# The Gram of a linear-attention kernel on two column halves of the array: groups of three heads, state in two PSUM banks

## The chip, the cores and the metric

The kernel runs on one core of one Trainium2 chip. The metric is the device time of one execution in microseconds (us), as the median of several. All executions quoted were with a granted TensorE clock of 1.0.

In this document PE is TensorE (matmul), PEld is TensorE's weight load, which overlaps PE, DVE is VectorE and ACT is ScalarE. "L434" is line 434 of the kernel that the profile belongs to. An edit shifts line numbers, so the Gram is L434 in the kernel before, L436 in the changed one.

## The reference, cut to what matters

Two branches of the same input x (2048 tokens, width 640) are mixed by a gate. Branch B is a feed-forward net (width 1728) with GELU. Branch A is linear attention with 32 heads of 20 channels:

```python
phi_q = concat([softmax(q @ w_phi), softmax(-q @ w_phi)])   # 40 features a head
phi_k = concat([softmax(k @ w_phi), softmax(-k @ w_phi)])
kv  = einsum("bhsf,bhsd->bhfd", phi_k, v)     # the state; summed over all tokens
z   = einsum("bhsf->bhf", phi_k)
num = einsum("bhqf,bhfd->bhqd", phi_q, kv)
den = einsum("bhqf,bhf->bhq", phi_q, z) + 1e-6
o   = num / den
```

The change concerns the state (kv, z), which the kernel calls the Gram: 16 tiles of 128 tokens, accumulated in PSUM.

## The kernel before

A one is appended to each head's 20 values, so v has 21 columns a head and z comes out with kv. `Ek` holds both halves of phi_k, `vaug` the values. Six heads (6 x 21 = 126 columns of v) form one group, and one matmul computes all 6 x 6 head pairs; only the diagonal blocks are of use. The rest is masked away later.

```python
NSE = 4        # slots of Ek
def gram_groups(self):
    fe = 6 * self.DH                                   # 120 features of six heads
    for g in range(6):
        lo = min(6 * g * self.DA, self.H * self.DA - P)
        yield g, 3 + g % 2 if g < 4 else 5, 2 * fe * (g // 2 if g < 4 else g - 4), lo, fe * g, min(fe, self.D - fe * g)

def gram(self, t):
    ...
    for g, b, c, lo, f0, nf in self.gram_groups():
        sc.op("pe", lambda e: e.matmul(
            self.bank(b)[:, c:c + 2 * nf], va[:, lo:lo + P], self.Ek[:, se, :, f0:f0 + nf],
            start=(t == 0 and g in (0, 1, 4)), stop=..., skip_group_check=True), ...)
```

One tile is six matmuls with weights 128x128: five stream 240 columns, one 80. They stand between other matmuls of the attention stage. The same loop issues key and value projections, `k_norm` on DVE (the softmax normalisation that the Gram needs), and the query projections `pq`:

```python
for t in range(4, NT):
    if t < 8: self.k_early(t, 1)
    else:     self.vk(t)
    self.k_norm(t)
    m = 2 * t - 2 if t < 8 else t + 5
    while n < m:
        if n == m - 1:
            for g in range(g, t - 2 if t < 8 else t - 1):
                self.gram(g)
            g = t - 2 if t < 8 else t - 1
        self.pq(order[n][0], order[n][1], n)
        n += 1
```

Tile 0's Gram is issued before this loop. The last two (14 and 15) stand among the first feed-forward matmuls. Tile 15 is followed by `kv_evac` (PSUM to SBUF, then a transposing DMA) and, three feed-forward chunks later, by `kv_mask` (DVE). `num` uses the result. Tiles 5 and 6 fall into the same iteration, so there are 15 bursts of Gram matmuls for 16 tiles.

The softmax here doesn't subtract the row's maximum and nothing guards it: scores larger than these inputs give would overflow.

Of the kernel before, what the change touches and what calls it, by code (L numbers as in the profile page):

```python
# [3 lines left out]
P = 128  # L4
# [101 lines left out]
class _Kernel:  # L106
# [314 lines left out]
                  reads=[("Rk", se)], writes=[("Ek", se, s)])  # L421

    def gram_groups(self):
        fe = 6 * self.DH
        for g in range(6):
            lo = min(6 * g * self.DA, self.H * self.DA - P)
            yield g, 3 + g % 2 if g < 4 else 5, 2 * fe * (g // 2 if g < 4 else g - 4), lo, fe * g, min(fe, self.D - fe * g)

    def gram(self, t):
        sc = self.sc  # L430
        se, sv = t % self.NSE, t % self.NSV
        va = self.vaug[:, sv, :, :].rearrange("p h c -> p (h c)")
        for g, b, c, lo, f0, nf in self.gram_groups():
            sc.op("pe", lambda e: e.matmul(  # L434
                self.bank(b)[:, c:c + 2 * nf], va[:, lo:lo + P], self.Ek[:, se, :, f0:f0 + nf],
                start=(t == 0 and g in (0, 1, 4)), stop=(t == self.NT - 1 and g in (2, 3, 5)), skip_group_check=True),  # L436
                reads=[("Ek", se, 0), ("Ek", se, 1), ("vaug", sv), ("vmain", sv), ("vone", sv)], writes=[("ps", b)],
                signal=(g in (2, 3, 5)))

    def kv_evac(self):  # L440
        sc = self.sc
        fe = 6 * self.DH

        def copy(ek, dst, src, rd, wr):
            if ek == "d":
                sc.op("dve", lambda e: e.tensor_copy(dst, src), reads=rd, writes=wr)
            else:
                sc.op("act", lambda e: e.activation(dst, src, AF.Copy), reads=rd, writes=wr)
        for pl, ek in ((0, "d"), (1, "a")):
            f = pl * fe  # L450
            dst = self.Ek[:, pl, :, 0:4 * fe].rearrange("p s (b c) -> p b s c", c=2 * fe)[:, :, :, f:f + fe]
            src = self.bank(3 + pl, 4 * fe).rearrange("p (b s f) -> p b s f", f=fe, s=2)
            copy(ek, dst, src, [("ps", 3 + pl)], [("Ek", pl, 0)])
        for pl, ek in ((0, "d"), (1, "d")):
            g = 4 + pl
            nf = min(fe, self.D - fe * g)
            src = self.bank(5)[:, pl * 2 * fe:pl * 2 * fe + 2 * nf].rearrange("p (s f) -> p s f", f=nf)
            copy(ek, self.Ek[:, pl, :, fe * g:fe * g + nf], src, [("ps", 5)], [("Ek", pl, 1)])
        for pl in (0, 1):
            sc.dma("sp", lambda e: e.dma_start_transpose(  # L460
                self.Ek[:, 2 + pl, :, :].rearrange("p s (i c) -> p (s i) c", c=P),
                self.Ek[:, pl, :, :].rearrange("p s f -> p (s f)")),
                reads=[("Ek", pl, 0), ("Ek", pl, 1)], writes=[("Ek", 2 + pl, 0), ("Ek", 2 + pl, 1)])

    def kv_mask(self):
        sc = self.sc
        self.kvk = {i: [] for i in range(self.KD)}
        lows = {g: lo for g, b, c, lo, f0, nf in self.gram_groups()}
        for i in range(self.KD):
            for g in range(self.HLO[i] // 6, self.HHI[i] // 6 + 1):  # L470
                h0, h1 = max(self.HLO[i], 6 * g), min(self.HHI[i], 6 * g + 5)
                nh, j0 = h1 - h0 + 1, h0 - self.HLO[i]
                o = i * P + h0 * self.DA - lows[g]
                dst = self.KV[:, i, :, j0 * self.DB:(j0 + nh) * self.DB].rearrange(
                    "p s (h c) -> p s h c", c=self.DB)[:, :, :, 0:self.DA]
                src = self.Ek[:, 2 + g % 2, :, o:o + nh * self.DA].rearrange("p s (h c) -> p s h c", c=self.DA)
                m = self.mask[:, i, j0:j0 + nh].unsqueeze(1).unsqueeze(3).to_broadcast([P, 2, nh, self.DA])
                sc.op("dve", lambda e: e.tensor_tensor(dst, src, m, ALU.mult),
                      reads=[("Ek", 2 + g % 2, 0), ("mask", i), ("KVd", i, 0), ("KVd", i, 1)], writes=[("KV", i, g)])
                self.kvk[i].append(("KV", i, g))  # L480

    def pq(self, b, i, n):
# [338 lines left out]
```

## Time and profile before

The median was 296.51 us over three runs (296.28 to 296.85).

| what | reading |
|---|---|
| PE busy, whole span | 98% |
| chain of waits | 93% PE |
| Gram's share of that chain | 3%, 15 bursts, 8.8 us |
| PE busy, 30 to 84 us | 54.00 of 54.00 us |

These are the engines' busy times on the page of the kernel before:

```profile
PE 291.0 (98%) x1904; PEld 169.1 (57%) x1904; DVE 162.7 (55%) x321; ACT 104.2 (35%) x183; POOL 27.8 (9%) x56
```

The chain of waits is the work that ended last, followed back from the last instruction, at each step to what released it. That of the kernel before, in order of time, follows: start in us, duration in us, engine, tile, line, number of instructions. L486 is `pq`, L341 the projections, L434 the Gram, L594 the feed-forward up-projections, L709 the output copy.

```profile
29.64 1.25 PE ps L486 x5
30.89 0.55 PE ps L434 x6
31.44 1.08 PE ps L486 x5
...
48.79 2.71 PE ps L341 x15
51.50 1.10 PE ps L434 x12
52.60 1.08 PE ps L486 x5
...
60.72 0.55 PE ps L434 x6
61.27 1.08 PE ps L486 x5
...
294.23 0.37 ACT outsb L709
```

From 29.64 us to the last output copy at 294.23 us, the chain is unbroken PE work (but for 0.02 us at its very end), 264.59 us long. Whatever the Gram saves there is saved in full, provided that nothing else becomes the limit. A tile costs 0.55 us (24 of these matmuls in a row took 2.19 us in experiment 3), so all 16 cost 8.76 us. A `pq` group after it takes 1.08 us, its ordinary duration.

The trace already holds matmuls in another tiling mode: the half chunk of the feed-forward (L672, weights of 64 rows, two at once on the array's row halves). These lines, again from the chain of the kernel before, price a change of mode. L699 is the output projection that follows.

```profile
119.86 0.38 PE ps L672 x4
120.24 1.46 PE ps L699 x10
...
125.93 1.36 PE ps L699 x10
...
172.98 0.65 PE ps L672 x8
```

Four more row-tiled matmuls cost 0.65 - 0.38 = 0.27 us, so a pair takes 0.135 us. The first two pairs therefore include 0.38 - 0.27 = 0.11 us for getting into the mode. The next ten full matmuls take 1.46 us in place of 1.36: another 0.10 us for getting out.

DVE's normalisation is close to being a second limit. In the timeline of DVE in the kernel before (start, duration, engine, line, operation, shapes), these are tile 6's two normalising multiplications:

```profile
50.19 1.56 DVE L420 TENSOR_TENSOR Ek<-Ek,Dk 128x640 bf16<-128x640 bf16 x2
```

They end at 51.75 us, and tile 6's Gram is the second half of the 1.10 us burst that starts at 51.50, so it starts at 52.05 us: 0.3 us of slack.

### The profile page before, as it was taken

How to read it: one execution, taken by the hardware profiler on the slowest of the kernel's cores; microseconds unless marked ns; L12 is line 12 of the kernel's file. 1: busy time of each engine (PE TensorE's matmuls, PEld its weight loads, DVE VectorE, ACT ScalarE, POOL GpSimd, SP SyncE). 2: the span in 40 equal slices, each digit the busy share in tenths (PEclk: the TensorE clock that was granted, in tenths of full speed). 3: DMA queues.
4: the chain of work that ended last, by engine and by line, in shares of the span. 5: the costliest groups of instructions: out<-in, count | busy, mean ns of one | idle time of the engine just before them, and what ended most of it. 6: DMA issues, size and time to landing. Idle time of an engine off the chain costs nothing.

```text
span 296.1 us, 4789 instructions
## 1 busy us (share of the span) xinstructions
PE 291.0 (98%) x1904; PEld 169.1 (57%) x1904; DVE 162.7 (55%) x321; ACT 104.2 (35%) x183; POOL 27.8 (9%) x56
## 2 busy tenths in 40 slices
PE   7989999999999999999999999999999999999997
PEld 3656565555554455766555567655556765555674
DVE  3238999998886579600777710077771007777100
ACT  3347787766773221112222211222221122222112
POOL 7000000000000011110111100012110001222000
PEclk9999999999999999999999999999999999999999
DMA  8999993000001302211011130101311000111111
GB/s 231 181 200 273 364 356 113 0 0 2 0 2 31 57 4 37 51 47 44 3 23 22 24 44 22 46 0 23 24 22 43 25 26 21 22 22 24 22 46 44
DMA packets 38224, 18.85 MB, mean 64 GB/s; under 512 B 30266, under 2 KB 37946, under 8 KB 38202
## 3 DMA queue, kind: packets, MB, share of 16 engines
q1 hardware_dynamic: 37392, 18.19, 25.0%
q10 hardware_dynamic: 810, 0.35, 0.4%
q8 instruction: 15, 0.25, 0.4%
q14 instruction: 7, 0.06, 0.1%
HBM read 9.04 MB, written 2.62 MB: 39 GB/s over the span
## 4 chain that ended last, share of the span: by engine, by line
PE 93%; SPq 3%; DMA 2%; ACT 1%; issue 0%; ACTq 0%
PE ps L594 38%; PE ps L693 19%; PE ps L341 12%; PE ps L699 8%; PE ps L486 7%; PE ps L630 4%; PE ps L434 3%; DMA xT<-in_A_x_dram 2%; SPq L213 2%; PE ps L604 1%; PE ps L672 1%; PE ps L321 1%; SPq L217 1%; SPq L226 1%; ACT Ek L400 0%; ACT Eq L492 0%
## 5 line engine op out<-in xcount | busy, mean ns | idle before, releaser
L599 DVE TENSOR_TENSOR hT<-ps,gl 128x512 bf16<-128x512 f32 x52 | 35.7, 688 | 79.8 <-PE ps L594 79.7
L594 PE MATMUL ps<-xT,wg_sb 128*128 128x512 bf16 x260 | 64.6, 379 | 0.0
L594 PE MATMUL ps<-xT,wu_sb 128*128 128x512 bf16 x260 | 64.6, 379 | 0.0
L597 ACT ACTIVATE gl<-ps 128x512 bf16<-128x512 f32 x52 | 31.1, 597 | 82.5 <-PE ps L594 80.3
L693 PE MATMUL ps<-wd_sb,hT 128*128 128x320 bf16 (+2 forms) x416 | 59.3, 299 | 0.0
L693 PEld LDWEIGHTS ps<-wd_sb,hT 128*128 128x128 bf16 x416 | 40.2, 98 | 16.8
L659 POOL TENSOR_TENSOR Og<-O,O 128x640 bf16<-128x640 bf16 x16 | 22.3, 1396 | 244.4 <-DVE O L657 244.4
L594 PEld LDWEIGHTS ps<-xT,wu_sb 128*128 128x128 bf16 x260 | 25.4, 98 | 30.7
L341 PE MATMUL ps<-w,xT 128*128 128x512 bf16 (+3 forms) x240 | 41.0, 321 | 1.4 <-DMA xT<-in_A_x_dram 1.4
L594 PEld LDWEIGHTS ps<-xT,wg_sb 128*128 128x128 bf16 x260 | 24.9, 98 | 26.4
L709 ACT ACTIVATE outsb<-ps,Gm 128x640 bf16<-128x640 f32 (+2 forms) x17 | 13.0, 763 | 71.5 <-PE ps L699 71.5
L341 PEld LDWEIGHTS ps<-w,xT 128*128 128x128 bf16 x240 | 22.3, 97 | 19.7 <-DMA xT<-in_A_x_dram 1.6
L411 DVE TENSOR_REDUCE Dk<-Ek 128x64 f32<-128x1280 bf16 x16 | 23.7, 1480 | 3.2 <-ACT gcol L403 3.2
L420 DVE TENSOR_TENSOR Ek<-Ek,Dk 128x640 bf16<-128x640 bf16 x32 | 25.0, 821 | 0.6
L486 PE MATMUL ps<-xT,wq 128*128 128x512 bf16 x100 | 24.7, 379 | 0.3 <-ACT Eq L492 0.3
L657 DVE TENSOR_TENSOR O<-ps,RH 128x640 bf16<-128x640 f32 x32 | 24.8, 815 | 0.0
L699 PE MATMUL ps<-wo_sb,goT 128*128 128x320 bf16 (+2 forms) x160 | 24.6, 299 | 0.0
L492 ACT ACTIVATE Eq<-ps 128x512 bf16<-128x512 f32 x40 | 21.7, 604 | 4.0 <-PE ps L486 4.0
L400 ACT ACTIVATE Ek<-ps 128x640 bf16<-128x640 f32 x32 | 20.7, 702 | 3.5 <-PE ps L341 3.5
L699 PEld LDWEIGHTS ps<-wo_sb,goT 128*128 128x128 bf16 x160 | 15.1, 98 | 7.2 <-issue 1.3
L630 PEld LDWEIGHTS ps<-KV,Eq 128*128 128x128 bf16 x192 | 12.0, 98 | 3.6
L630 PE MATMUL ps<-KV,Eq 128*128 128x154 bf16 x192 | 13.7, 221 | 0.0
(63 smaller groups left out, 148.4 us busy)
## 6 DMA issues: line engine op xcount, KB each, us to landing
out_dram<-outsb SPq DMA_DIRECT2D x15, 160.0 KB, 1.8
wd_sb<-in_B_w_down_dram SPq DMA_DIRECT2D x1, 2080.0 KB, 13.7
wg_sb<-in_B_w_gate_dram SPq DMA_DIRECT2D x1, 1120.0 KB, 6.1
wu_sb<-in_B_w_up_dram SPq DMA_DIRECT2D x1, 1120.0 KB, 8.5
wg_sb<-in_B_w_gate_dram SPq DMA_DIRECT2D x1, 960.0 KB, 9.8
wu_sb<-in_B_w_up_dram SPq DMA_DIRECT2D x1, 960.0 KB, 10.2
w<-in_A_wqkv_dram SPq DMA_DIRECT2D x5, 160.0 KB, 4.2
wo_sb<-in_A_wo_dram SPq DMA_DIRECT2D x1, 800.0 KB, 9.2
```

The costliest lines, as they stand in the source:

```text
L341: sc.op("pe", lambda e, kt=kt: e.matmul(self.bank(bank)[:, bcol:bcol + n], self.xT[:, kt, t * P:(t + 1) * P], self.w3[:, kt, c0:c0 + n], s ...
L411: sc.op("dve", lambda e: e.tensor_reduce(self.Dk[:, se, 0, :].rearrange("p (s h) -> p s h", h=H), self.Ek[:, se, :, :].rearrange("p s (h d ...
L420: sc.op("dve", lambda e, v=v, r=r: e.tensor_tensor(v, v, r, ALU.mult), reads=[("Rk", se)], writes=[("Ek", se, s)])
L486: sc.op("pe", lambda e, kt=kt: e.matmul(self.bank(bank), self.wq2[:, kt, i * P:(i + 1) * P], self.xT[:, kt, b * self.BT:(b + 1) * self.BT] ...
L594: sc.op("pe", lambda e, kt=kt, w=w, bk=bk: e.matmul(self.bank(bk), w[:, kt, c * P:(c + 1) * P], xs(kt), start=(kt == 0), stop=(kt == self. ...
L597: sc.op("act", lambda e: e.activation(self.gl[:, slot, :], self.bank(banks[0]), AF.Gelu_apprx_tanh), reads=[("ps", banks[0])], writes=[("g ...
L599: sc.op("dve", lambda e: e.tensor_tensor(self.hT[:, c, :], self.bank(banks[1]), self.gl[:, slot, :], ALU.mult), reads=[("ps", banks[1]), ( ...
L630: sc.op("pe", lambda e, s=s, i=i, n=n, o0=o0, k0=k0, bk=bk, r=r: e.matmul(self.bank(bk)[:, o0:o0 + n], self.Eq[:, s, i, t * P:(t + 1) * P] ...
L657: dve(lambda e, o=o, f=f, s=s: e.tensor_tensor(o, V[s][:, :, :, 0:DH], f, ALU.mult), rb + [key(6 + s)], [("O", s, sl)], guard=old)
L659: sc.op("pool", lambda e: e.tensor_tensor(self.Og[:, sl, :], self.O1[:, sl, :], self.O2[:, sl, :], ALU.add), reads=[("O", 0, sl), ("O", 1, ...
L693: sc.op("pe", lambda e: e.matmul(self.bank(bk, w), self.hT[:, c, tt * P:(tt + 1) * P], self.wd_sb[:, c, w0:w0 + w], start=(c == 0 and not ...
L699: sc.op("pe", lambda e: e.matmul(self.bank(bk, w), self.goT[:, gs, k, :], self.wo_sb[:, k, w0:w0 + w], start=False, stop=(k == self.KD - 1 ...
```

## The change

A group is now three heads: 3 x 21 = 63 columns of v, so its weights fit one half of the array's columns (128x64). Even groups write PSUM partitions 0 to 63, odd groups 64 to 127, and two run at once. Fewer unwanted head pairs are computed: a tile streams 5 x 120 + 80 = 680 columns (each pair counted once) instead of 5 x 240 + 80 = 1280. The state needs two banks instead of three, one transposing DMA instead of two, and 15 mask operations instead of 10. The core of the diff, with cuts:

```diff
 def gram_groups(self):
-    fe = 6 * self.DH
-    for g in range(6):
-        lo = min(6 * g * self.DA, self.H * self.DA - P)
-        yield g, 3 + g % 2 if g < 4 else 5, ..., lo, fe * g, min(fe, self.D - fe * g)
+    fe = 3 * self.DH
+    for g in range(11):
+        u = g // 2
+        yield (g, 64 * (g % 2), 3 + u // 4, 2 * fe * (u % 4), min(3 * g * self.DA, self.H * self.DA - 64), fe * g,
+               min(fe, self.D - fe * g))
 def gram(self, t):
-    for g, b, c, lo, f0, nf in self.gram_groups():
+    for g, a, b, c, lo, f0, nf in self.gram_groups():
         sc.op("pe", lambda e: e.matmul(
-            self.bank(b)[:, c:c + 2 * nf], va[:, lo:lo + P], self.Ek[:, se, :, f0:f0 + nf],
+            self.ps[a:a + 64, b * 512 + c:b * 512 + c + 2 * nf], va[:, lo:lo + 64], self.Ek[:, se, :, f0:f0 + nf],
 ...
 def kv_evac(self):           # 4 copies, 2 transposing DMAs -> 2 copies on DVE + 3 on ACT, 1 DMA
 ...
 def kv_mask(self):           # 10 multiplications of up to six heads -> 15 of up to three
-    for g in range(self.HLO[i] // 6, self.HHI[i] // 6 + 1):
+    for g in range(self.HLO[i] // 3, self.HHI[i] // 3 + 1):
```

More of the change, by code (lines that the diff above doesn't have):

```diff
@@ L423, in gram_groups @@
     def gram_groups(self):
-        fe = 6 * self.DH
-        for g in range(6):
-            lo = min(6 * g * self.DA, self.H * self.DA - P)
-            yield g, 3 + g % 2 if g < 4 else 5, 2 * fe * (g // 2 if g < 4 else g - 4), lo, fe * g, min(fe, self.D - fe * g)
+        fe = 3 * self.DH
[3 more added lines that the diff above has]
+                   min(fe, self.D - fe * g))
     def gram(self, t):
@@ L432, in gram, with copy @@
         va = self.vaug[:, sv, :, :].rearrange("p h c -> p (h c)")
-        for g, b, c, lo, f0, nf in self.gram_groups():
+        for g, a, b, c, lo, f0, nf in self.gram_groups():
             sc.op("pe", lambda e: e.matmul(
-                self.bank(b)[:, c:c + 2 * nf], va[:, lo:lo + P], self.Ek[:, se, :, f0:f0 + nf],
-                start=(t == 0 and g in (0, 1, 4)), stop=(t == self.NT - 1 and g in (2, 3, 5)), skip_group_check=True),
+                self.ps[a:a + 64, b * 512 + c:b * 512 + c + 2 * nf], va[:, lo:lo + 64], self.Ek[:, se, :, f0:f0 + nf],
+                start=(t == 0 and g in (0, 1, 8, 9)), stop=(t == self.NT - 1 and g in (6, 7, 9, 10)),
+                skip_group_check=True),
                 reads=[("Ek", se, 0), ("Ek", se, 1), ("vaug", sv), ("vmain", sv), ("vone", sv)], writes=[("ps", b)],
-                signal=(g in (2, 3, 5)))
+                signal=(g in (7, 10)))
     def kv_evac(self):
         sc = self.sc
-        fe = 6 * self.DH
-        def copy(ek, dst, src, rd, wr):
+        fe = 3 * self.DH
+        def copy(ek, dst, src, b):
+            rd, wr = [("ps", b)], [("Ek", 0, 0), ("Ek", 0, 1)]
             if ek == "d":
@@ L448, in copy @@
                 sc.op("act", lambda e: e.activation(dst, src, AF.Copy), reads=rd, writes=wr)
-        for pl, ek in ((0, "d"), (1, "a")):
-            f = pl * fe
-            dst = self.Ek[:, pl, :, 0:4 * fe].rearrange("p s (b c) -> p b s c", c=2 * fe)[:, :, :, f:f + fe]
-            src = self.bank(3 + pl, 4 * fe).rearrange("p (b s f) -> p b s f", f=fe, s=2)
-            copy(ek, dst, src, [("ps", 3 + pl)], [("Ek", pl, 0)])
-        for pl, ek in ((0, "d"), (1, "d")):
-            g = 4 + pl
-            nf = min(fe, self.D - fe * g)
-            src = self.bank(5)[:, pl * 2 * fe:pl * 2 * fe + 2 * nf].rearrange("p (s f) -> p s f", f=nf)
-            copy(ek, self.Ek[:, pl, :, fe * g:fe * g + nf], src, [("ps", 5)], [("Ek", pl, 1)])
-        for pl in (0, 1):
-            sc.dma("sp", lambda e: e.dma_start_transpose(
-                self.Ek[:, 2 + pl, :, :].rearrange("p s (i c) -> p (s i) c", c=P),
-                self.Ek[:, pl, :, :].rearrange("p s f -> p (s f)")),
-                reads=[("Ek", pl, 0), ("Ek", pl, 1)], writes=[("Ek", 2 + pl, 0), ("Ek", 2 + pl, 1)])
+        for q in (0, 1):
+            a, z = 64 * q, 64 * q + 64
+            dst = self.Ek[a:z, 0, :, 0:8 * fe].rearrange("p s (u q f) -> p u s q f", q=2, f=fe)[:, :, :, q, :]
+            src = self.ps[a:z, 3 * 512:3 * 512 + 8 * fe].rearrange("p (u s f) -> p u s f", s=2, f=fe)
+            copy("d", dst, src, 3)
+        for g, a, b, c, lo, f0, nf in self.gram_groups():
+            if b == 4:
+                src = self.ps[a:a + 64, b * 512 + c:b * 512 + c + 2 * nf].rearrange("p (s f) -> p s f", f=nf)
+                copy("a", self.Ek[a:a + 64, 0, :, f0:f0 + nf], src, b)
+        sc.dma("sp", lambda e: e.dma_start_transpose(
+            self.Ek[:, 2, :, :].rearrange("p s (i c) -> p (s i) c", c=P),
+            self.Ek[:, 0, :, :].rearrange("p s f -> p (s f)")),
+            reads=[("Ek", 0, 0), ("Ek", 0, 1)], writes=[("Ek", 2, 0), ("Ek", 2, 1)])
     def kv_mask(self):
@@ L467, in kv_mask @@
         self.kvk = {i: [] for i in range(self.KD)}
-        lows = {g: lo for g, b, c, lo, f0, nf in self.gram_groups()}
+        lows = {g: lo for g, a, b, c, lo, f0, nf in self.gram_groups()}
         for i in range(self.KD):
-            for g in range(self.HLO[i] // 6, self.HHI[i] // 6 + 1):
-                h0, h1 = max(self.HLO[i], 6 * g), min(self.HHI[i], 6 * g + 5)
+            for g in range(self.HLO[i] // 3, self.HHI[i] // 3 + 1):
+                h0, h1 = max(self.HLO[i], 3 * g), min(self.HHI[i], 3 * g + 2)
                 nh, j0 = h1 - h0 + 1, h0 - self.HLO[i]
-                o = i * P + h0 * self.DA - lows[g]
+                o = i * P + 64 * (g % 2) + h0 * self.DA - lows[g]
                 dst = self.KV[:, i, :, j0 * self.DB:(j0 + nh) * self.DB].rearrange(
                     "p s (h c) -> p s h c", c=self.DB)[:, :, :, 0:self.DA]
-                src = self.Ek[:, 2 + g % 2, :, o:o + nh * self.DA].rearrange("p s (h c) -> p s h c", c=self.DA)
+                src = self.Ek[:, 2, :, o:o + nh * self.DA].rearrange("p s (h c) -> p s h c", c=self.DA)
                 m = self.mask[:, i, j0:j0 + nh].unsqueeze(1).unsqueeze(3).to_broadcast([P, 2, nh, self.DA])
                 sc.op("dve", lambda e: e.tensor_tensor(dst, src, m, ALU.mult),
-                      reads=[("Ek", 2 + g % 2, 0), ("mask", i), ("KVd", i, 0), ("KVd", i, 1)], writes=[("KV", i, g)])
+                      reads=[("Ek", 2, 0), ("mask", i), ("KVd", i, 0), ("KVd", i, 1)], writes=[("KV", i, g)])
                 self.kvk[i].append(("KV", i, g))
```

## The prediction

> **What bounds it now.** TensorE. The page gives PE 98% busy, a granted clock of nine tenths or more everywhere, and the chain of waits is 93% PE. From 30 us to the end the chain is one unbroken run of PE pieces. The Gram line (L434) is 3% of that chain: 15 bursts for 16 tiles, each of six matmuls (five of 240 columns, one of 80) in 0.55 us, so 8.8 us in all. That is 1280 columns at 2.33 columns per ns, i.e. streaming at full rate with the weight loads hidden. The whole stake is therefore 8.8 us of 296.
>
> **What the change does to PE.** Per tile, 11 matmuls of 128x64 weights (ten of 120 columns, one of 80) replace six. If both column halves run together, a tile streams 5x120+80 = 680 columns: 0.28 to 0.30 us, 0.25 us less, 4 us in all. The array also has to change from 128x128 to two column tiles and back in each burst. The Trainium skill, "TensorEngine Tiling (Array Packing)", Key Properties, says that changing the tiling mode drains TensorE, and its Restrictions say that column tiling disables fast weight load. This trace has a comparable switch, the row-tiled half chunk (L672): in block 0, four matmuls of 64x320 take 0.38 us and eight in later blocks 0.65 us, so a pair costs 0.135 us (320 columns, truly concurrent) and entering 0.11 us; the first wo piece after it takes 1.46 us against 1.36, so leaving costs 0.10 us. Before both, the weight loads sit idle 0.26 us ("issue"). So a burst pays about 0.21 us for the switches: 15 x 0.21 = 3.2 us. Estimate: 3.2 + 16 x 0.30 = 8.0 us against 8.8, a gain of 0.8 us. If the 64-column loads without the fast path hold a pair at 0.07 us rather than 0.05, the gain is gone; if loads of the two halves are serial, a burst costs about 0.8 us and the kernel loses 4 us.
>
> **A cap on the upside.** VectorE's normalisation runs gaplessly from 26 to 60 us, 3.58 us a tile. Tile 6's ends at 51.75 us and its Gram starts at about 52.05. So before that point PE can get ahead only about 0.3 us, whatever the first Grams save. Even with free switches the gain is about 0.3 + 10 x 0.27 = 3 us, not 4.
>
> **Off the critical path.** Evacuation: VectorE 2 copies of 64x480 (before: 3 copies, 1.11 us), ScalarE three small ones instead of one of 0.57 us. One transposing DMA instead of two (3.4 us to landing). The mask goes from 10 to 15 smaller operations, same elements: 2.35 us becomes an estimated 2.8 us. The masked state is ready at 102.1 us, first used at 103.3 us, so about 0.8 us of slack stays. A freed PSUM bank is reused by nothing.
>
> **Prediction.** 296.0 us, 293.7 to 298.8 eight times in ten; faster by over 2%: 0.01, within 2%: 0.95, slower by over 2%: 0.04.
>
> **What would show it.** Right: in the chain, Gram bursts of 0.45 to 0.57 us including the longer piece after each; new PEld idle labelled "issue" of about 0.25 us before and after each burst; weight loads 128x64; PE otherwise without gaps from 30 us on; no wait at the first use of the state. Wrong: bursts near 0.3 us with no longer piece after them (switch nearly free; then a short wait of PE for VectorE before tile 6's Gram), or bursts of 0.7 us or more (the halves do not overlap, or weight loads are serial).
>
> **What would make it wrong.** The switch cost is taken from row tiling, and column tiling may differ; the load rate of 64-column weights is not in this trace; eleven short matmuls with their loads may meet an issue floor.

## The result, and the profile after

The changed kernel took 295.94 us (median of 4 runs, 295.58 to 296.58) against 296.39 us (4 runs, 296.14 to 296.85). Ratios here are the mean time of one kernel's fast runs over that of the other's of the same rounds, so they are not quite the ratio of the medians. This ratio is 0.9985, 95% interval 0.9965 to 1.0005: the same, at the 2% mark. Experiment 1 repeats it with more runs.

The whole time is a poor scale for a few tenths of a microsecond. The 30 us before the chain's unbroken PE stretch differ from run to run: the stretch starts at 29.64 us in the trace before and at 28.26 us in the trace after, 1.38 us earlier. The change touches nothing before that point. So this document also measures the *PE stretch*: from the start of the third `pq` group, which waits for ACT, to the start of the last output copy. The changed kernel was profiled twice and gave 264.18 and 264.19 us. The kernel before gave 264.59, and its regrouped variant in experiment 3 the same 264.59. On this scale the gain is 0.41 us.

The engines' busy times on the page of the changed kernel:

```profile
PE 290.7 (99%) x1984; PEld 165.2 (56%) x1984; DVE 163.3 (55%) x325; ACT 104.2 (35%) x185; POOL 27.7 (9%) x56
```

The chain of waits of the changed kernel in order of time, at the places shown of before (L488 is `pq`, L436 the Gram, L711 the output copy):

```profile
28.26 1.25 PE ps L488 x5
29.51 0.42 PE ps L436 x11
29.93 1.19 PE ps L488 x5
...
47.29 2.71 PE ps L341 x15
49.99 0.42 PE ps L436 x11
50.41 0.07 issue
50.48 0.46 PE ps L436 x11
50.94 1.19 PE ps L488 x5
...
59.14 0.42 PE ps L436 x11
...
292.44 0.37 ACT outsb L711
```

A burst went from 0.55 to 0.42 us, but the `pq` group after it went from 1.08 to 1.19 us. Together they cost 0.53 us against 0.55. The busy share of PE doesn't tell this story: it reads 98% and 99%.

The line-by-line view of the Gram in the changed kernel (duration in ns as minimum/median/maximum, first and last start, shapes; the third line is the idle time of PEld before its loads):

```profile
L436 PEld LDWEIGHTS ps<-Ek,vaug x176: 106/109/111, 29.4 to 90.5; 128*64 128x64 bf16 x176
L436 PE MATMUL ps<-Ek,vaug x176: 198/215/242, 29.4 to 90.6; 128*64 128x120 bf16 x160, 128*64 128x80 bf16 x16
  issue: 3.0, 10
```

The array is in 128*64 tiles there. PEld sits idle ahead of the bursts for 3.0 us put down to "issue" (time in which the profile shows nothing that the engine waited for), plus 1.8 us that the same view puts down to DVE instructions. These names say little: in the timeline, seven of the sixteen sets of loads come after 0.42 us of idle time, eight after 0.21 and one (tile 6's) after 0.18, whichever name it is given. In the kernel before, that view shows no idle time for the Gram's loads.

The double burst is the place that the prediction called a cap. DVE in the timeline of the changed kernel, with the two sets of the Gram's loads:

```profile
49.56 0.82 DVE L420 TENSOR_TENSOR Ek<-Ek,Dk 128x640 bf16<-128x640 bf16 x1
49.92 0.35 PEld L436 LDWEIGHTS ps<-Ek,vaug 128*64 128x64 bf16 x11 [0.21 <-DVE Ek L420]
50.45 0.35 PEld L436 LDWEIGHTS ps<-Ek,vaug 128*64 128x64 bf16 x11 [0.18 <-DVE Ek L420]
```

Tile 6's normalisation ends at 49.56 + 0.82 = 50.38 us, and its Gram's first load starts at 50.45. The chain above gives this wait as 0.07 us of "issue". Tile 6 waited for DVE, and experiment 12 shows what that cost.

The off-path parts behaved. In the timelines, the lines of mask and first use are, before:

```profile
99.80 2.35 DVE L478 TENSOR_TENSOR KV<-Ek,mask 128x252 bf16<-128x252 bf16 x10
103.31 0.85 PE L630 MATMUL ps<-KV,Eq 128*128 128x154 bf16 x12
```

and after:

```profile
98.01 2.69 DVE L480 TENSOR_TENSOR KV<-Ek,mask 128x126 bf16<-128x126 bf16 x15
101.52 0.85 PE L632 MATMUL ps<-KV,Eq 128*128 128x154 bf16 x12
```

The mask takes 0.34 us longer and ends at 100.70 us, 0.8 us before PE uses it. PE waits for nothing there, in either kernel.

### The profile page after: what moved, and what is told of

It reads as the page before. It is cut to its first block, busy times and chain, and to the rows that moved or that the text cites. A ratio compares the mean times of both kernels' runs of the same rounds, so it can differ in the third digit from the quotient of the medians.

```text
span 294.3 us, 4951 instructions
## 1 busy us (share of the span) xinstructions
PE 290.7 (99%) x1984; PEld 165.2 (56%) x1984; DVE 163.3 (55%) x325; ACT 104.2 (35%) x185; POOL 27.7 (9%) x56
## 4 chain that ended last, share of the span: by engine, by line
PE 97%; DMA 1%; ACT 1%; issue 0%; ACTq 0%
PE ps L596 38%; PE ps L695 19%; PE ps L341 13%; PE ps L701 8%; PE ps L488 7%; PE ps L632 4%; PE ps L436 2%; PE ps L350 2%; PE ps L606 1%; DMA xtok<-in_A_x_dram 1%; PE ps L321 1%; PE ps L674 1%; PE ps L280 0%; ACT Ek L400 0%; ACT Eq L494 0%; ACT outsb L711 0%
## 5 line engine op out<-in xcount | busy, mean ns | idle before, releaser
L711 ACT ACTIVATE outsb<-ps,Gm 128x640 bf16<-128x640 f32 (+2 forms) x17 | 13.0, 762 | 71.5 <-PE ps L701 71.5
L488 PE MATMUL ps<-xT,wq 128*128 128x512 bf16 x100 | 24.8, 381 | 0.3 <-ACT Eq L494 0.3
L488 PEld LDWEIGHTS ps<-xT,wq 128*128 128x128 bf16 x100 | 8.6, 98 | 9.2 <-ACT Eq L494 0.8
```

Of the source, the lines that this page charges most:

```text
L488: sc.op("pe", lambda e, kt=kt: e.matmul(self.bank(bank), self.wq2[:, kt, i * P:(i + 1) * P], self.xT[:, kt, b * self.BT:(b + 1) * self.BT] ...
```

## The experiments

Theory 1: the pairs run at full rate, but each entry into and exit from the column-tiled mode costs PE a fixed time, about 0.22 us, and one tile per burst is too little work to repay it. Rival A: the cost lies in every matmul, because the loads are slow or an issue floor holds. Rival B: weights narrower than 128 columns are slow in themselves, whatever the mode. Each run was timed beside the kernel before on the same chip.

| run | bursts | median us | ratio to before (95%) | PE stretch us |
|---|---|---|---|---|
| before | 15 | 296.39 | 1 | 264.59 |
| 1 changed, again | 15 | 296.28 | 0.9981 (0.9962 to 1.0) | 264.19 |
| 2 changed, merged | 4 | 293.62 | 0.9888 (0.9868 to 0.9907) | 261.49 |
| 3 before, merged | 4 | 296.63 | 0.9992 (0.9975 to 1.001) | 264.59 |
| 4 changed, Gram twice | 15 | 300.22 | 1.0119 (1.0098 to 1.0139) | 268.73 |
| 5 before + tiny 128x64 | 15 | 300.53 | 1.0147 (1.013 to 1.0164) | 268.26 |
| 6 before + tiny 128x128 | 15 | 296.96 | 1.0023 (1.0006 to 1.004) | 264.99 |
| 7 changed, one half only | 15 | 300.12 | 1.0126 (1.0107 to 1.0146) | 267.89 |
| 8 before, weights 128x96 | 15 | 296.2 | 0.9994 (0.9977 to 1.0011) | 264.60 |
| 9 changed, seven bursts | 7 | 294.15 | 0.9927 (0.9913 to 0.9941) | 262.16 |
| 10 changed, three bursts | 3 | 293.48 | 0.9902 (0.9888 to 0.9916) | 261.27 |
| 11 changed, even then odd | 15 | 297.42 | 1.0042 (1.0025 to 1.0058) | 265.46 |
| 12 changed, tile 6 later | 15 | 295.71 | 0.996 (0.9944 to 0.9977) | 263.95 |

The results of 7 and 8 are wrong on purpose; all others are correct. The medians of the kernel before in the four groups of runs (1 to 4, 5 to 8, 9 to 11, 12) were 296.8, 296.21, 296.25 and 296.82 us.

### 1. The changed kernel again

No edit.

> The changed kernel once more, with more rounds, to size the gain. From the two traces the Gram takes 15 x (0.42 + 0.11) + 0.46 + 0.07 = 8.5 us against 8.8 us, so both theories expect 0.3 to 0.5 us less than before: a ratio of 0.9983 to 0.999.

The ratio was 0.9981, just outside the expected 0.9983 to 0.999 but well within the noise, and the PE stretch was 0.40 us shorter than before. As expected: a gain, and a tiny one. The interval of the whole time still touches 1.0.

### 2. Fewer bursts

```diff
-    NSE = 4
+    NSE = 8
+    BURSTS = {7: (0, 1, 2, 3), 10: (4, 5, 6, 7), 13: (8, 9, 10, 11)}
 ...
-                    for g in range(g, t - 2 if t < 8 else t - 1):
+                    for g in self.BURSTS.get(t, ()):
                         self.gram(g)
-                    g = t - 2 if t < 8 else t - 1
```

(the calls for tiles 0, 14 and 15 go, and tiles 12 to 15 are issued where tile 15 was)

> The changed kernel with the 16 tiles' Grams in 4 bursts of four tiles instead of 15 bursts, and 8 slots for Ek instead of 4. Theory 1 (a fixed cost of about 0.22 us for each entry into and exit from the column-tiled mode eats the gain): 11 bursts less x 0.22 = 2.4 us less than the changed kernel, and the 0.15 us wait for VectorE in tile 6's Gram goes too; about 293.2 us, ratio to before 0.990; in the trace a burst of 44 matmuls takes about 0.11 + 4 x 0.29 = 1.3 us. Rival (the cost is in every pair: slow 64-column weight loads or an issue floor): a burst of 44 takes 4 x 0.42 = 1.7 us and the time falls by 0.5 us at most.

The time was 293.62 us, ratio 0.9888. One burst in its chain of waits, with the `pq` group after it:

```profile
56.15 1.31 PE ps L437 x43
57.46 1.19 PE ps L489 x5
```

Four tiles took 1.31 us (44 matmuls; one record is missing from the chain), so each tile after the first costs (1.31 - 0.42) / 3 = 0.30 us. Rival A, which wanted 1.7 us, is out. The stretch fell by 2.7 us against the changed kernel.

### 3. The control of 2

The same edit on the kernel before.

> The control: the kernel before with the same regrouping into 4 bursts and 8 slots. Both theories: no mode change is saved there, so the time stays within 0.3 us of before (ratio 0.999 to 1.001). If it gets faster too, the gain of the merged changed kernel is not from the mode switches.

Nothing moved: ratio 0.9992, and the stretch 264.59 us as before. One burst in its chain:

```profile
57.78 2.19 PE ps L435 x24
```

So the gain of experiment 2 is not from the slots or from where the bursts stand; full-array bursts gain nothing by merging.

### 4. Twice the Gram in each burst

```diff
-        for g, a, b, c, lo, f0, nf in self.gram_groups():
+        for rep, (g, a, b, c, lo, f0, nf) in [(r, x) for r in (0, 1) for x in self.gram_groups()]:
 ...
```

(the flags start, stop and signal are set at the first and the last repetition)

> The changed kernel with each tile's 11 Gram matmuls issued twice in a row, within the same burst (numerator and denominator both double, so the result is still right). Theory 1 (fixed cost per burst, pairs at full streaming rate): 680 columns more per tile, 16 x 0.29 = 4.6 us more than the changed kernel, less whatever slack there is. Rival (cost in every pair): 16 x 0.42 = 6.7 us more or above.

The stretch grew by 268.73 - 264.18 = 4.55 us (the medians by 3.9 us), near 4.6 and far from 6.7. The double burst and a single one in the chain:

```profile
51.57 1.31 PE ps L436 x43
...
56.77 0.71 PE ps L436 x22
57.49 1.19 PE ps L488 x5
```

A second tile costs 0.71 - 0.42 = 0.29 us, and the exit still costs 0.11. Within a burst, 11 matmuls with their loads run at practically the streaming time of 680 columns (0.29 us at 2.37 columns per ns, the rate of the kernel before's 512-column matmuls: five in 1.08 us). The double burst is one piece here (44 matmuls in 1.31 us, one record missing): its first tile now lasts long enough for tile 6's data to be ready, and the wait that the changed kernel has there is gone. That alone saves 0.23 us (experiment 12), so the second tiles cost (4.55 + 0.23) / 16 = 0.30 us each.

### 5. The mode switch alone

```diff
+        sc.op("pe", lambda e: e.matmul(
+            self.ps[0:64, 5 * 512 + 400:5 * 512 + 408], va[:, 0:64], self.Ek[:, se, :, 0:4],
+            start=False, stop=False, skip_group_check=True), ...)
         for g, b, c, lo, f0, nf in self.gram_groups():
```

> The kernel before with one tiny matmul (8 columns, weights 128x64, so in the column-tiled mode) put ahead of each tile's six full-array Gram matmuls; its output goes to unused columns. It measures the mode switches by themselves: 16 entries and exits. Theory 1: 16 x 0.22 = 3.5 us more than before plus 16 x about 0.03 us of the matmul itself, about 4 us in all. Rival (no cost of the switch as such): under 0.6 us.

The kernel before got 3.67 us longer on the stretch (4.3 us in the medians) from 16 matmuls of eight columns. One of them in the chain, with the six full-array matmuls after it:

```profile
62.07 0.12 PE ps L433
62.20 0.65 PE ps L439 x6
62.85 1.08 PE ps L491 x5
```

Entering costs 0.12 us with the matmul itself; the six Gram matmuls after it take 0.65 us in place of 0.55.

### 6. The control of 5

The same tiny matmul with weights `va[:, 0:128]` and 128 output partitions.

> The control of the run before it: the same tiny matmul with weights 128x128, so without a change of mode. Both theories: 16 x 0.03 = 0.5 us or less over the kernel before.

The stretch grew by 0.40 us only. In the chain, the same place:

```profile
60.30 0.01 PE ps L433
60.30 0.57 PE ps L439 x6
```

Going in and out of the mode thus costs (268.26 - 264.99) / 16 = 0.20 us, measured by itself. The first part of theory 1 stands.

### 7. Only one half of the columns

```diff
         for g, a, b, c, lo, f0, nf in self.gram_groups():
+            a = a if t == 0 else 0
```

> The changed kernel with, from the second tile on, every group on the lower half of the columns (wrong result on purpose): same mode switches, same matmuls, no two at once. If the pairs ran concurrently in the changed kernel, as the burst of 0.42 us says, the 11 matmuls now stream one after another, 1280 columns: 15 x 0.25 = 3.8 us more than the changed kernel, about 300 us. If the halves never overlapped, no change.

A burst went from 0.42 to 0.68 us, and the stretch grew by 3.71 us. The pairs of the changed kernel did run at once. The streaming time is really nearly halved (680 columns for 1280); it is the switch that takes it back. One burst in the chain:

```profile
56.95 0.68 PE ps L437 x11
57.63 1.19 PE ps L489 x5
```

### 8. Narrow weights without a mode change

```diff
+        w = P if t == 0 else 96
 ...
-                self.bank(b)[:, c:c + 2 * nf], va[:, lo:lo + P], self.Ek[...]
+                self.ps[0:w, b * 512 + c:b * 512 + c + 2 * nf], va[:, lo:lo + w], self.Ek[...]
```

> The kernel before with, from the second tile on, Gram weights of 128x96 instead of 128x128 (wrong result on purpose): the array stays whole, so no mode switch, but the weights are narrower than 128 columns, as the changed kernel's are. Theory 1: no cost, within 0.4 us of before, and no idle weight load around the bursts. Rival (weights of fewer than 128 columns load slowly and that is what the changed kernel pays): 1 to 4 us more, with bursts clearly over 0.55 us.

Its line-by-line view of the weight loads, and one burst in its chain:

```profile
L435 PEld LDWEIGHTS ps<-Ek,vaug x96: 97/123/125, 29.7 to 91.6; 128*96 128x96 bf16 x90, 128*128 128x128 bf16 x6
```

```profile
59.96 0.55 PE ps L435 x6
```

A load of 96 columns takes 123 ns where one of 128 takes 98 in the kernel before, so these narrower weights do load more slowly. It cost nothing: the loads hide behind the matmuls, the burst stays at 0.55 us and the stretch at 264.60. Rival B is out for 96 columns by this run. Weights of 64 columns were never run outside the column-tiled mode; for them experiments 2 and 4 speak, where a further tile costs only its streaming time. The profile names this shape's tile 128*96, but whatever that means inside, it shows no cost of entering or leaving.

### 9 and 10. Doses: seven and three bursts

As in 2, with six slots and the bursts (0, 1), (2, 3), (4, 5), (6, 7, 8), (9, 10), (11, 12), (13, 14, 15); and with eight slots and (0 to 4), (5 to 10), (11 to 15).

> The changed kernel with its Grams in 7 bursts (of two, two, two, three, two, two and three tiles) and 6 slots for Ek: a dose between the 15 bursts of the changed kernel and the 4 of the merged one. Theory 1 (0.22 us per burst): 8 bursts less, 1.8 us less than the changed kernel, and 0.15 us of tile 6's wait; about 294.4 us, ratio to before about 0.9925. Rival (the merged kernel gained from its 8 slots or from when the bursts stand, not from their number): no such proportion.

> The changed kernel with its Grams in 3 bursts (five, six and five tiles) and 8 slots, the fewest that the slots allow. Theory 1: one burst less than the merged kernel, 0.2 us; ratio to before 0.987 to 0.990, in the trace bursts of about 1.6 and 1.9 us and no wait of TensorE before them.

The times were 294.15 and 293.48 us. On the stretch, 7, 4 and 3 bursts gave 262.16, 261.49 and 261.27 us: 0.22 us a burst, exactly in proportion. Between three and four bursts the whole time can't tell: the ratios are 0.9902 and 0.9888, taken beside different runs of before, with overlapping intervals. The three bursts took 1.61, 1.91 and 1.61 us, as expected; the ratio of experiment 10 is just above the expected 0.987 to 0.990. The longest burst in its chain:

```profile
65.06 1.91 PE ps L437 x65
```

(66 matmuls, one record missing.) Both kernels beat the kernel before and the changed one.

### 11. All even groups first, then all odd ones

```diff
-        for g, a, b, c, lo, f0, nf in self.gram_groups():
+        for g, a, b, c, lo, f0, nf in sorted(self.gram_groups(), key=lambda x: x[0] % 2):
 ...
```

(the signal moves from group 10 to group 9, which is now the last)

> The changed kernel with each tile's groups issued as all those of the lower half first, then all those of the upper half. If two matmuls run at once only when neighbours in the instruction stream go to different halves, this loses nearly what one half alone lost: 3 to 4 us more than the changed kernel, bursts of about 0.66 us. If the array sorts out the halves across several instructions, no change.

Neither expectation held: bursts of 0.52 us, between 0.42 (alternating) and 0.68 (one half), and a stretch 1.28 us longer than the changed kernel's. In the chain:

```profile
46.45 0.52 PE ps L436 x11
...
50.86 0.82 PE ps L436 x22
```

In the double burst the second tile adds 0.30 us, as with alternating order. So matmuls of different halves overlap across several instructions. Presumably a burst that begins with six of the same half runs partly alone, but that was not tested. How far the overlap reaches, and what limits it, was not measured. Of the two, alternating is the better order.

### 12. Tile 6 where its data is ready

```diff
-    NSE = 4
+    NSE = 5
+    BURSTS = {4: (1,), 5: (2,), 6: (3,), 7: (4,), 8: (5,), 9: (6, 7), 10: (8,), ..., 15: (13,)}
```

> The changed kernel with tile 6's Gram moved from the burst of tile 5 into that of tile 7, one iteration later, and 5 slots for Ek; still 15 bursts. Theory 1: in the changed kernel tile 6's Gram waited for VectorE and so paid a second entry (0.46 + 0.07 us instead of about 0.30); with the data ready the pair of tiles takes about 0.71 us in one burst and the stretch from 30 us to the end gets 0.2 us shorter. Rival (a second tile in a burst always costs what the first does): no difference. The whole time is too noisy to show 0.2 us; the verdict is read from the trace.

The pair in the chain:

```profile
55.79 0.71 PE ps L437 x22
```

The pair took 0.71 us in place of 0.42 + 0.07 + 0.46, and the stretch was 263.95 us, 0.23 less than the changed kernel's. So the wait for DVE was only 0.07 us, but it cost 0.23 us, as much as one more entry and exit. No change of mode was part of it, as all 22 loads of the changed kernel's double burst are in 128*64 tiles: besides the wait, tile 6 took 0.46 us where a second tile without a wait takes 0.30. The full array shows the same: in the kernel before, the first `pq` group of the stretch, which starts after a wait for ACT, takes 1.25 us where the others take 1.08. In both places the piece after a wait was 0.16 to 0.17 us longer.

## Why the prediction was right or wrong

The time (296.0 predicted, 295.94 measured) and the class (within 2%) were right, and the mechanism was the one the prediction gave. That the time was hit to 0.06 us is luck: the same changed kernel gave 296.28 us in experiment 1, and the medians of the kernel before lay between 296.21 and 296.82. The gain, which is what was argued, came out at half of the estimate.

- *PE bounds the kernel, and the stake is 8.8 us.* Right: 16 x 0.55 = 8.8 us, and everything saved there shows in the stretch.
- *The halves run together.* Right: a tile within a burst costs 0.30 us (experiments 2 and 4), and without the second half 0.26 us more (experiment 7).
- *About 0.21 us for entering and leaving, taken from the row-tiled bursts.* Right in size: 0.20 us by itself (experiments 5 and 6), 0.22 us per burst by dose (2, 9, 10). That row tiling and column tiling cost the same was an assumption; it now has numbers.
- *A gain of 0.8 us.* Mis-sized: it was 0.41 us. The terms put in at 15 x 0.21 + 16 x 0.30 came out as if 16 x 0.22 + 16 x 0.30. The term that was too small is "15 x 0.21 = 3.2 us": it counted one entry per burst, and the double burst cost as much as two. The prediction had seen the cause ("before that point PE can get ahead only about 0.3 us") but used it only as a cap on a large gain and left it out of the central estimate. In fact a burst's first tile, now 0.13 us shorter, used that slack up with the few hundredths saved by each burst before, PE waited 0.07 us, and tile 6 lost 0.23 us in all. The prediction had named such a short wait only as a sign of being wrong, for switches that are nearly free. Taking that away returned 0.23 us (experiment 12). The rest is 0.01 to 0.02 us a burst.
- *Loads 128x64, PEld idle about 0.25 us before and after each burst.* Right before, in kind (0.21 us for half of the sets of loads, 0.42 us for most others); wrong after: the view gives the `pq` loads no idle time of this kind, and the exit shows only as a longer `pq` piece.
- *Evacuation and mask are off the path, with about 0.8 us of slack.* Right: 0.8 us.

The count of it all, with n the number of entries: 16 x 0.299 + n x 0.224 us, against 8.76 us before. For n = 16 (the changed kernel, tile 6's wait counted as one more entry) that is 8.37 us, a gain of 0.39; measured 0.41. For n = 4 it is 5.68 us, a gain of 3.08; measured 3.10. For experiment 12, n = 15, it is a gain of 0.62; measured 0.64. The two constants were read from these same runs, so this is a check that they fit together, not a new test.

The intent was sound: 0.55 - 0.30 = 0.25 us saved a tile. The place was wrong: 0.22 us of it went for a mode change around each single tile. Merged into three or four bursts, which takes only more slots of `Ek`, the same matmuls gain about 3 us, or 1%.

What stays open: how much of the 0.22 us is draining the array and how much is the first weight load, which no longer runs ahead under the matmuls before it (a load lasts 109 ns, and PEld idles 0.21 or 0.42 us before it). No run here separates the two. Experiments 5 and 6 show that the change of mode brings the cost, but no run shows whether it costs more than any other break in the flow of loads and matmuls: the wait of tile 6, without a change of mode, cost as much (experiment 12).

## What to carry to other kernels

Price a tiled burst as a fixed entry and exit (here 0.22 us) plus its streaming time, and look at what follows the burst as well as at the burst: half of the cost sat in the next piece. Before halving a small group of matmuls by tiling, gather the groups so that several share one entry, and make sure that the data of all of them is ready, because a short wait inside the burst can cost as much as another entry (here 0.23 us for a wait of 0.07). Where two halves should run at once, alternate them in the instruction stream (here 0.42 us a burst against 0.52).

## What the Trainium skill lacked or had wrong

- "TensorEngine Tiling (Array Packing)", Key Properties, says that changing the tiling mode drains TensorE, without a figure. Here going in and out cost 0.20 us by itself and 0.22 us per burst by dose; that it is a drain, no run here shows.
- The same page, "Theoretical Speedup", gives up to 2x for a dimension of at most 64. Within a burst it was 0.55 to 0.30 us, 1.8x (by the columns, 1280 to 680, 1.9x); with the switch around every tile 0.55 to 0.53 us.
- The same page, Restrictions, says that column tiling disables fast weight load, but gives no figure there. A 128x64 load in the tiled mode took 109 ns against 98 for 128x128 in the full array; 11 of them overlapped and were done in 0.35 us, without holding up the pairs. Whether the full array's loads took the fast path, no run here shows.
- "TensorE: Matmul & The Clock Gate", "LDWEIGHTS (loading the stationary operand)", gives the time as the number of columns over 1.2 in ns, so 53, 80 and 107 ns for 64, 96 and 128 columns. The durations in the trace were 109, 123 and 98 ns: they do not follow that rule. (Loads overlap, so a duration in the trace need not be what a load adds.)
- The same page, Part 3, tells of tiles running at once, but not what the order of the halves in the stream is worth. Alternating the halves gave bursts of 0.42 us, even groups before odd ones 0.52 us (experiment 11).
